# Split weights w1 and w2: the second difference on ScalarE and GpSimd instead of VectorE

## The chip, the cores and the metric

The kernel runs on one core of a Trainium2 chip. The core has TensorE (PE in the profile; PEld is its weight load), VectorE (DVE), ScalarE (ACT), GpSimd (POOL) and SyncE (SP, which here only issues DMAs); GpSimd issues DMAs too. Each engine works off its own queue in order and waits for others by semaphores. The metric is device time of one execution, in microseconds (us); lower is better.

## The reference, cut to what matters

A gated linear recurrence per batch and head makes a state and an output y; the outputs, heads side by side, go through a feed-forward block without nonlinearity.

```python
# batch 4, heads 8, seq 768, head_dim 48; d_model 384, d_ff 1024
scale = np.minimum(mag, 0.999) / (mag + 1e-06)          # mag = |a|
for t in range(S):
    new_re = ar * S_re - ai * S_im
    new_im = ar * S_im + ai * S_re
    S_re, S_im = (new_re + kv, new_im)                  # kv = outer(k_t, v_t)
    y[:, :, t] = np.einsum('bhd,bhde->bhe', q[:, :, t], S_re)
...
a = x @ w1
b = x @ w2
h = a * b @ w3
return h @ w_out
```

## The kernel before

The 3072 tokens are cut into eight units of 384 (unit u is half of batch u // 2). For a unit the kernel works out the gates (`gates`, `gates_apart`: logarithms, exponentials, scans over time, arctangent, sine and cosine, on ScalarE and VectorE in turn), multiplies them into k and q (gR, k, gA, q: the names of the tiles), and moves the results by DMA into KL and QL, where real and imaginary parts lie beneath each other. Then come, per chunk of 128 tokens, transposes (`turn`, tile tp, copied to KT by ScalarE), the state's products (`state`, tile kv, summed into T), the scores (`scores`, tile sc, copied to A under a mask) and the outputs (`outputs`, tile y). The state's products wait for both KT copies of their chunk. The feed-forward of a unit (`ffn_ab`, tiles m and ab; `ffn_out`, tiles o and ot; w3o is w3 times w_out, made once) runs on TensorE between the pieces of the next unit. In ffn_ab each of eight column blocks ends in one product of a and b on VectorE (L1105, called an ab product below).

For units 0 to 2, x times w1 and w2 is done in full float32. For units 3 to 7 x, w1 and w2 are each cut into two words of a faster type (float32r), and a product is done as heads, tails and a correction by differences. The weights are cut once, in `split_ops`, while unit 3 is worked on and unit 2's feed-forward ends: for each of eight blocks i a head (wh, ScalarE, L1152), a tail (low[:, 0], VectorE, L1155) and a difference (low[:, 1], VectorE, L1157). A head is written into the room of the block before it (ws), so it waits for that block's tail. x is cut in `outputs` (x0 on ScalarE, x1 on VectorE, x2 on GpSimd, L1051).

The order of instructions on ScalarE, VectorE, GpSimd and SP in most of the program is set by a planner that runs when the program is built: `run` walks through TensorE's list, and `fill` takes the next piece of the gates, of the weights' cutting or of the input checks where a clock for each engine, kept from the costs in the `yield` lines, says that it fits. The costs are only for the planner. What has been planned stands in each engine's queue in that order. GpSimd's queue also holds the checks of the inputs (`check_weights`; tiles look, seen, looked), of which those left at the end are tested on VectorE and counted by TensorE shortly before the last outputs, and the DMAs of k, q and vr for the next unit. The gates' im is loaded by SP's queue, after the moves' first part for the unit before.

The planner's rule for the cutting:

```python
while (splitting and splitting[0][0] and gate["u"] > THREE and split_t[0] < whole[0] // 2 * 2 and
       start(splitting[0][0]) <= clock["PE"] + 4.0):
    split_next()
while looks and ("ab", 0, KF - 1) in last and clock["POOL"] < min(clock["PE"], split_at(k) - HOLD):
    clock["POOL"] = max(clock["POOL"], clock["PE"] - 4.0) + next(looks[0], 1e9)
```

Of the kernel before, what the change touches and what calls it, by code (L numbers as in the profile page):

```python
# [17 lines left out]
AF = mybir.ActivationFunctionType  # L18
OP = mybir.AluOpType
# [359 lines left out]
def kernel(  # L379
# [36 lines left out]
    nc = tc.nc  # L416
# [22 lines left out]
    TOP, BITS = 1.0 - 2.0 ** -13, 2.0 ** 12  # L439
# [702 lines left out]
    def split_ops():  # L1142
        which = [(n, m) for n in range(FF // WB) for m in (1, 0)]
        for i, (n, m) in enumerate(which):
            yield "ACT", 0.85, ("head", i), (("tail", i - 1),) if i else ()
            w = w_t[n][m]
            if i:
                h = w12.tile([P, KD, WB], FR, tag="w%d%d" % which[i - 1], name="wh")
            else:
                h = late[0].tile([P, KD, WB], FR, tag="x0", padded_shape=[P, KD, TT], name="wh")  # L1150
            w3_h[n, m] = h
            nc.scalar.activation(out=h, in_=w, func=AF.Copy, scale=TOP * BITS)  # L1152
            L = w3_l[n, m] = late[0].tile([P, 2, KD, WB], FR, tag=f"low{n}{m}", name="low")
            yield "DVE", 1.12, ("tail", i), (("head", i),)
            nc.vector.scalar_tensor_tensor(out=L[:, 0], in0=w, scalar=BITS, in1=h, op0=OP.mult, op1=OP.subtract)  # L1155
            yield "DVE", 1.12, ("diff", i), (("tail", i),)
            nc.vector.scalar_tensor_tensor(out=L[:, 1], in0=h, scalar=1.0 / BITS, in1=L[:, 0], op0=OP.mult, op1=OP.subtract)  # L1157
            if i == len(which) - 1:
                yield "ACT", 0.85, ("head", 0), (("tail", i),)
                h = w12.tile([P, KD, WB], FR, tag="w%d%d" % which[i], name="wh")  # L1160
                nc.scalar.activation(out=h, in_=w3_h[which[0]], func=AF.Copy)
                w3_h[which[0]] = h
            split_t[0] += 1
# [573 lines left out]
    with tc.manual_schedule(engines={mybir.EngineType.PE}):  # L1737
# [32 lines left out]
        with tc.manual_schedule(engines={mybir.EngineType.Activation, mybir.EngineType.DVE, mybir.EngineType.Pool, mybir.EngineType.SP}):  # L1770

            paced.append(True)
            clock.update(PE=0.0, ACT=0.0, DVE=0.0, POOL=0.0, SP=3.0, DMA=8.0)
            landings[:] = [0.0] * RING
            ready.clear()
            ready.update({"moves": 9.0, ("raw", 0): 0.0, ("re", 1): 2.0})
            w12_load(0, slice(len(got) and got[0][0][0].stop, KD))
            turn_v(0)
            w12_load(1)
            rest = ffn(0)  # L1780
            urgent.append([None, w12_ops()])

            def head(i):
                if i % 4 == 0:
                    force(i // 4)
                rest[i][1]()
                if i == HEAD - 1:
                    phase.close()
                    late.append(fast.enter_context(tc.tile_pool(name="late", bufs=1)))
                    late.append(fast.enter_context(tc.tile_pool(name="looks", bufs=1)))  # L1790
                    looks.append(check_weights(late[1]))
                    ops = split_ops()
                    splitting.append([next(ops), ops])
            seq = mixed([x for p in pieces(0) for x in p], fills, FILLS[0]) + [("begin", 0)] + [(rest[i][0], lambda i=i: head(i)) for i in range(HEAD)]
            for u in range(1, NU):
                seq += unit(u, rest[HEAD:] if u == 1 else ffn(u - 1), AHEAD[u])
            seq += ffn(NU - 1)
            advance()
            run(seq[:-4] + [("judge", 0)] + seq[-4:-2] + [("judge", 1)] + seq[-2:])
# [41 lines left out]
```

## Time and profile before

| | |
|---|---|
| three timed executions | 534.25, 535.98, 538.77 us; median 535.98 |
| the profiled execution, first to last instruction | 534.5 us (its own device time isn't listed apart from this) |
| mean granted clock of TensorE | 0.993 |
| busy: TensorE, VectorE, ScalarE, GpSimd | 93%, 70%, 61%, 48% |
| the cutting of w1 and w2 | 158 to 180 us |

A row of a timeline gives start, length, engine, line, operation, what is written from what, and in brackets how long the engine had been idle and which work ended that. A line of the page's fifth part gives count, busy time, mean duration and idle time before. Lengths on an engine can overlap by about 0.1 us, since the next instruction starts while the last one drains.

### The profile page before, as it was taken

How to read it: one execution, taken by the hardware profiler on the slowest of the kernel's cores; microseconds unless marked ns; L12 is line 12 of the kernel's file. 1: busy time of each engine (PE TensorE's matmuls, PEld its weight loads, DVE VectorE, ACT ScalarE, POOL GpSimd, SP SyncE). 2: the span in 40 equal slices, each digit the busy share in tenths (PEclk: the TensorE clock that was granted, in tenths of full speed). 3: DMA queues.
4: the chain of work that ended last, by engine and by line, in shares of the span. 5: the costliest groups of instructions: out<-in, count | busy, mean ns of one | idle time of the engine just before them, and what ended most of it. 6: DMA issues, size and time to landing. Idle time of an engine off the chain costs nothing.

```text
span 534.5 us, 13643 instructions
## 1 busy us (share of the span) xinstructions
PE 498.3 (93%) x5594; PEld 378.1 (71%) x5594; DVE 374.7 (70%) x607; ACT 325.6 (61%) x569; POOL 254.0 (48%) x317
## 2 busy tenths in 40 slices
PE   5689889999998999988999999999999998999995
PEld 2355565556655679957888688967896787878972
DVE  7999699855779988756773876577657837336750
ACT  6979866665675458982587557855786554213420
POOL 1000000028968886752664765487457458415510
PEclk9899999999999999998999999999999999999999
DMA  8999859692379219791599239932993176716611
GB/s 258 369 400 286 189 161 307 126 232 72 79 174 229 73 56 234 157 219 40 126 236 216 77 82 245 225 90 70 229 232 87 40 209 169 205 43 189 200 50 37
DMA packets 66424, 89.75 MB, mean 168 GB/s; under 512 B 29872, under 2 KB 53872, under 8 KB 65584
## 3 DMA queue, kind: packets, MB, share of 16 engines
q1 hardware_dynamic: 57904, 59.15, 44.0%
q0 software_dynamic: 8448, 29.63, 20.3%
q8 instruction: 46, 0.75, 0.6%
q14 instruction: 26, 0.21, 0.1%
HBM read 61.01 MB, written 4.72 MB: 123 GB/s over the span
## 4 chain that ended last, share of the span: by engine, by line
PE 51%; DVE 17%; DMA 13%; issue 6%; ACT 5%; POOL 5%; SPq 1%; POOLq 0%; DVEq 0%; ACTq 0%
PE m L1089 24%; PE o L1184 16%; PE y L1043 4%; PE sc L1004 4%; DMA k<-in_k_dram 3%; DMA KL<-k 3%; PE kv L1069 2%; DVE gR L750 2%; PE tp L991 2%; DMA QL<-q 2%; DMA q<-in_q_dram 2%; DMA look<-in_a_re_dram 1%; DVE gA L753 1%; DMA raw<-in_w_dram 1%; POOL look L1327 1%
## 5 line engine op out<-in xcount | busy, mean ns | idle before, releaser
L1184 PE MATMUL o<-w3o,ab 128*128 128x384 f32 x384 | 131.7, 492 | 0.0
L1089 PE MATMUL m<-x,low 128*128 128x384 f32 x576 | 119.2, 339 | 0.0
L1089 PEld LDWEIGHTS m<-x,low 128*128 128x128 f32 x576 | 102.6, 188 | 0.2 <-ACT m L1123 0.2
L1184 PEld LDWEIGHTS o<-w3o,ab 128*128 128x128 f32 x384 | 70.4, 190 | 45.6 <-issue 2.4
L1105 DVE TENSOR_TENSOR ab<-m,ab 128x384 f32<-128x384 f32 x64 | 35.1, 553 | 57.2 <-PE m L1089 39.4
L1089 PE MATMUL m<-x,wh 128*128 128x384 f32 x288 | 69.6, 350 | 3.4 <-ACT ab L1130 2.4
L1123 ACT ACTIVATE m<-m 128x384 f32<-128x384 f32 x96 | 45.5, 476 | 36.0 <-PE m L1089 35.6
L1089 PE MATMUL m<-xT,ws 128*128 128x384 f32 x192 | 63.1, 487 | 1.2 <-ACT xT L1054 1.2
L1328 POOL TENSOR_SCALAR look<-look 128x192 f32<-128x192 f32 (+1 forms) x55 | 54.4, 988 | 5.0
L1089 PEld LDWEIGHTS m<-x,wh 128*128 128x128 f32 x288 | 50.8, 188 | 7.4 <-ACT ab L1130 3.6
L1325 POOL TENSOR_TENSOR look<-look 128x256 f32<-128x256 f32 (+1 forms) x43 | 31.9, 743 | 50.1 <-DMA look<-in_w_dram 32.3
L1089 PEld LDWEIGHTS m<-xT,ws 128*128 128x128 f32 x192 | 36.0, 190 | 25.6 <-ACT xT L1054 1.7
L1273 POOL MEMSET seen<- 128x256 bf16 x1 | 0.3, 317 | 107.7 <-DVE ab L1105 107.7
L1007 DVE COPY_PREDICATED A<-mask,sc 128x512 f32<-128x512 uint8 x48 | 32.8, 734 | 26.5 <-PE sc L1004 26.5
L1289 POOL TENSOR_TENSOR seen<-seen,look 128x192 bf16<-128x192 bf16 (+1 forms) x55 | 44.3, 805 | 4.5
L1051 POOL TENSOR_TENSOR x<-x,x 128x384 fp32r<-128x384 f32 x18 | 23.1, 1284 | 41.7 <-DVE x L1050 41.5
L1188 ACT COPY ot<-o 128x384 f32<-128x384 f32 x24 | 11.4, 476 | 48.4 <-PE o L1184 48.2
L1043 PE MATMUL y<-A,V 128*32 128x128 f32 x768 | 40.2, 276 | 0.6 <-issue 0.6
L1004 PEld LDWEIGHTS sc<-QL,KL 96*32 96x32 f32 x1536 | 29.2, 112 | 13.6 <-issue 8.7
L1004 PE MATMUL sc<-QL,KL 96*32 96x32 f32 (+3 forms) x1536 | 32.8, 238 | 4.4 <-DMA QL<-q 3.0
L1043 PEld LDWEIGHTS y<-A,V 128*32 128x32 f32 x768 | 35.0, 112 | 1.5 <-issue 1.5
L1043 PE MATMUL y<-QL,T 96*32 96x128 f32 x640 | 35.6, 275 | 0.0
(163 smaller groups left out, 909.2 us busy)
## 6 DMA issues: line engine op xcount, KB each, us to landing
looked<-in_w_dram POOLq DMA_DIRECT2D x14, 512.0 KB, 4.5
look<-in_w_dram POOLq DMA_DIRECT2D x27, 256.0 KB, 5.0
raw<-in_w_dram SPq DMA_DIRECT2D x6, 1024.0 KB, 10.3
KL<-gR SPq DMA_DIRECT2D x24, 192.5 KB, 3.6
KL<-k SPq DMA_DIRECT2D x24, 192.5 KB, 7.1
QL<-gA SPq DMA_DIRECT2D x24, 192.0 KB, 8.2
QL<-q SPq DMA_DIRECT2D x24, 192.0 KB, 7.9
raw<-in_w_dram SPq DMA_DIRECT2D x6, 768.0 KB, 6.1
```

Of the source, the lines that this page charges most:

```text
L1004: nc.tensor.matmul(out=sc[SB * g:SB * g + SB, j, s0:C], lhsT=KL[:, x * n + j, w][:, s0:s0 + SB], rhs=QL[:, x * n + j, w][:, s0:C], start=T ...
L1007: last["sc", u, c, x] = nc.vector.copy_predicated(out=A[:, x * n:(x + 1) * n], data=sc, mask=mask)
L1043: nc.tensor.matmul(out=o, lhsT=a, rhs=b, start=s0, stop=s1)
L1051: nc.gpsimd.tensor_tensor(out=x[2], in0=x[1], in1=x[0], op=OP.subtract)
L1089: nc.tensor.matmul(out=out, lhsT=a, rhs=b, start=start and i == 0, stop=i == len(terms) - 1, skip_group_check=not start)
L1105: last["ab", u, j] = nc.vector.tensor_tensor(out=ab_t[u][:, j], in0=m, in1=ab_t[u][:, j], op=OP.mult)
L1123: nc.scalar.activation(out=got[m], in_=got[m], func=AF.Copy, scale=1.0 + 1.0 / BITS)
L1184: nc.tensor.matmul(out=m, lhsT=ab_t[u][:, f, t * P:(t + 1) * P], rhs=w3o[:, f], start=(f == 0), stop=(f == KF - 1))
L1188: nc.scalar.copy(out=o, in_=m)
L1289: nc.gpsimd.tensor_tensor(out=seen[:, 0:n], in0=seen[:, 0:n], in1=x, op=OP.add)
L1325: tt(out=x, in0=x, in1=x, op=OP.mult)
L1328: ts(out=x, in0=x, scalar1=low, scalar2=None, op0=OP.is_ge)
```

## The change

The difference low[:, 1], which is head / 2^12 minus tail, was one VectorE instruction. Now ScalarE writes head / 2^12 into low[:, 1], and GpSimd subtracts the tail from it in place. The planner gets a cost for each (0.85 for ScalarE, 2.6 for GpSimd), in place of 1.12 for VectorE, and so plans the work around it anew.

```diff
             nc.scalar.activation(out=h, in_=w, func=AF.Copy, scale=TOP * BITS)
             L = w3_l[n, m] = late[0].tile([P, 2, KD, WB], FR, tag=f"low{n}{m}", name="low")
+            yield "ACT", 0.85, ("small", i), (("head", i),)
+            nc.scalar.activation(out=L[:, 1], in_=h, func=AF.Copy, scale=1.0 / BITS)
             yield "DVE", 1.12, ("tail", i), (("head", i),)
             nc.vector.scalar_tensor_tensor(out=L[:, 0], in0=w, scalar=BITS, in1=h, op0=OP.mult, op1=OP.subtract)
-            yield "DVE", 1.12, ("diff", i), (("tail", i),)
-            nc.vector.scalar_tensor_tensor(out=L[:, 1], in0=h, scalar=1.0 / BITS, in1=L[:, 0], op0=OP.mult, op1=OP.subtract)
+            yield "POOL", 2.6, ("diff", i), (("tail", i), ("small", i))
+            nc.gpsimd.tensor_tensor(out=L[:, 1], in0=L[:, 1], in1=L[:, 0], op=OP.subtract)
```

TensorE's order stays as it was, instruction for instruction; that of the others moves. Lines from 1155 on have other numbers in the changed program: a small copy is L1155, a tail L1157, a subtraction L1159, and what follows has two more than before.

VectorE in the cutting. Before, its end: the last two tails (L1155), each followed by its difference (L1157), with a sum into the state T between, and then the first product of the gates of unit 4 (im by re):

```order
L1155 SCALAR_TENSOR_TENSOR low<-ws,wh 128x768
L1157 SCALAR_TENSOR_TENSOR low<-wh,low 128x768
L1075 TENSOR_TENSOR T_123<-kv,T_122 96x8x48
L1155 SCALAR_TENSOR_TENSOR low<-ws,wh 128x768
L1157 SCALAR_TENSOR_TENSOR low<-wh,low 128x768
L645 TENSOR_TENSOR im<-im,re 128x384
```

VectorE in the changed program, the beginning of the cutting (L1157 is a tail here):

```order
L1105 TENSOR_TENSOR ab<-m,ab 128x384
L1157 SCALAR_TENSOR_TENSOR low<-ws,wh 128x768
L645 TENSOR_TENSOR im<-im,re 128x384
L1157 SCALAR_TENSOR_TENSOR low<-ws,wh 128x768
L1105 TENSOR_TENSOR ab<-m,ab 128x384
L1157 SCALAR_TENSOR_TENSOR low<-ws,wh 128x768 x2
```

The gates' first product has moved from behind the eighth tail to behind the first.

ScalarE in the same place, before, from the second head (L1152) to the second KT copy, with ab copies (L1101) between:

```order
L1152 ACTIVATE wh<-ws 128x768
L1101 COPY ab<-m 128x384
L1152 ACTIVATE wh<-ws 128x768
L993 COPY KT<-tp 128x128x3
L1101 COPY ab<-m 128x384
L1152 ACTIVATE wh<-ws 128x768
L993 COPY KT<-tp 128x128x3
```

and in the changed program, with the small copies (L1155):

```order
L1152 ACTIVATE wh<-ws 128x768
L1101 COPY ab<-m 128x384
L1155 ACTIVATE low<-wh 128x768
L1152 ACTIVATE wh<-ws 128x768
L1155 ACTIVATE low<-wh 128x768
L993 COPY KT<-tp 128x128x3
L1101 COPY ab<-m 128x384
L1152 ACTIVATE wh<-ws 128x768
L1155 ACTIVATE low<-wh 128x768
L993 COPY KT<-tp 128x128x3
```

The two KT copies stand behind the same heads as before, and each behind one small copy more of the block at hand. The same copies, with the last ones, stand later for the third chunk.

GpSimd. Before, between the loads of k, q and vr for unit 3 and those for unit 4, nine checks of the inputs stood ahead of x2 of unit 3; the last of them and what follows:

```order
L1325 TENSOR_TENSOR look<-look 128x256
L1328 TENSOR_SCALAR look<-look 128x256
L1289 TENSOR_TENSOR seen<-seen,look 128x256
L1051 TENSOR_TENSOR x_1880<-x_1879,x_1878 128x3x128 x3
L527 DMA k<-in_k_dram 128x3x384
L527 DMA q<-in_q_dram 128x3x384
L569 DMA vr<-in_v_dram 128x3x384
```

In the changed program four checks stand there, the end of the fourth here, and then the eight subtractions (L1159):

```order
L1332 TENSOR_TENSOR look<-look 128x192
L1291 TENSOR_TENSOR seen<-seen,look 128x192
L1159 TENSOR_TENSOR low<-low 128x768 x8
L1051 TENSOR_TENSOR x_1867<-x_1866,x_1865 128x3x128 x3
L527 DMA k<-in_k_dram 128x3x384
L527 DMA q<-in_q_dram 128x3x384
L569 DMA vr<-in_v_dram 128x3x384
```

Five checks have moved behind the loads for unit 4, and so all later ones back; at the program's end 13 groups of w3's words are left behind the last x2 instead of 11.

VectorE in unit 4, where the gates' angles are summed (L686) and k is scaled (L702), as the difference of the two programs (- before, + changed):

```order
-L686 SCALAR_TENSOR_TENSOR gZ<-im,st_ang 128x384
-L1105 TENSOR_TENSOR ab<-m,ab 128x384
-L686 SCALAR_TENSOR_TENSOR gZ<-im,st_ang 128x384 x2
-L1105 TENSOR_TENSOR ab<-m,ab 128x384
+L686 SCALAR_TENSOR_TENSOR gZ<-im,st_ang 128x384 x3
 L691 COPY st_ang<-gZ 128x9
 L702 TENSOR_TENSOR k<-k,gR 128x384
```

The gates of unit 4 stand two ab products earlier: five ab products were ahead of the first product for the moves (L750, gR from k), three are now.

## Rows read from the trace of the kernel before

**Rows 1.** The page, its head and part 1

```profile
span 534.5 us, 13643 instructions
...
PE 498.3 (93%) x5594; PEld 378.1 (71%) x5594; DVE 374.7 (70%) x607; ACT 325.6 (61%) x569; POOL 254.0 (48%) x317
...
```

**Rows 2.** Timeline of TensorE, 150 to 262 us: start, length, instruction, idle time before

```profile
...
164.74 2.10 PE L1089 MATMUL m<-xT,ws 128*128 128x384 f32 x6
169.01 0.88 PE L1069 MATMUL kv<-vr,KT 128*32 128x48 f32 x48 [2.17 <-ACT KT L993]
...
174.50 0.88 PE L1069 MATMUL kv<-vr,KT 128*32 128x48 f32 x48
...
181.28 0.88 PE L1069 MATMUL kv<-vr,KT 128*32 128x48 f32 x48
...
235.75 2.85 PE L1184 MATMUL o<-w3o,ab 128*128 128x384 f32 x8
241.58 1.32 PE L1004 MATMUL sc<-QL,KL 96*32 96x128 f32 x64 [2.98 <-DMA QL<-q]
...
```

**Rows 3.** Stretches of 1 us, TensorE alone: length, busy, granted clock, DMA share, GB/s

```profile
...
243.00:244.00 1.00, 0.79 (x29) 0.72 0.00 0
244.00:245.00 1.00, 1.00 (x40) 0.50 0.00 0
...
246.00:247.00 1.00, 1.00 (x31) 0.57 0.08 16
...
```

**Rows 4.** SP's issues, DMA landings around each (last number), and VectorE's timeline

```profile
...
161.31 1.06 SPq L527 DMA_DIRECT2D im<-in_a_im_dram  x1
...
im<-in_a_im_dram SPq DMA_DIRECT2D x1, 576.0 KB, 7.2
...
223.54 0.60 SPq L527 DMA_DIRECT2D im<-in_a_im_dram  x1
...
im<-in_a_im_dram SPq DMA_DIRECT2D x1, 576.0 KB, 8.9
...
232.54 0.56 DVE L645 TENSOR_TENSOR im<-im,re 128x384 f32<-128x384 f32 x1 [0.72 <-DMA im<-in_a_im_dram]
...
```

**Rows 5.** Timeline of VectorE, 150 to 260 us, and line L1157 with its durations

```profile
...
161.85 0.94 DVE L1155 SCALAR_TENSOR_TENSOR low<-ws,wh 128x768 fp32r<-128x768 f32 x1
...
163.99 1.30 DVE L1155 SCALAR_TENSOR_TENSOR low<-ws,wh 128x768 fp32r<-128x768 f32 x1
...
179.97 0.69 DVE L645 TENSOR_TENSOR im<-im,re 128x384 f32<-128x384 f32 x1
...
L1157 DVE SCALAR_TENSOR_TENSOR low<-wh,low x8: 943/980/1235, 162.8 to 179.1; 128x768 fp32r<-128x768 f32 x8
...
```

**Rows 6.** Timeline of ScalarE, 150 to 260 us

```profile
...
167.67 0.84 ACT L1152 ACTIVATE wh<-ws 128x768 fp32r<-128x768 f32 x1 [0.71 <-DVE low L1155]
168.42 0.54 ACT L993 COPY KT<-tp 128x384 f32<-128x384 f32 x1
...
```

**Rows 7.** Timeline of GpSimd, 140 to 320 us, and line L1051 (min/median/max ns)

```profile
...
163.32 1.15 POOL L1289 TENSOR_TENSOR seen<-seen,look 128x192 bf16<-128x192 bf16 x1
...
L1051 POOL TENSOR_TENSOR x<-x,x x18: 989/1066/1663, 193.8 to 480.5; 128x384 fp32r<-128x384 f32 x18
...
```

**Rows 8.** The page, part 5, VectorE's products for ab

```profile
...
L1105 DVE TENSOR_TENSOR ab<-m,ab 128x384 f32<-128x384 f32 x64 | 35.1, 553 | 57.2 <-PE m L1089 39.4
...
```

**Rows 9.** Timeline of VectorE, 150 to 260 us, gates of unit 4

```profile
...
213.26 0.54 DVE L1105 TENSOR_TENSOR ab<-m,ab 128x384 f32<-128x384 f32 x1
...
219.92 0.68 DVE L750 TENSOR_TENSOR gR<-k,re 128x384 f32<-128x384 f32 x1
...
```

**Rows 10.** Timelines of GpSimd and VectorE at the end

```profile
...
508.23 1.04 POOL L1358 TENSOR_TENSOR looked<-looked 128x512 f32<-128x512 f32 x1 [1.54 <-DMA looked<-in_w_dram]
511.20 1.04 POOL L1358 TENSOR_TENSOR looked<-looked 128x512 f32<-128x512 f32 x1 [1.93 <-DMA looked<-in_w_dram]
...
523.17 0.15 DVE L1481 SCALAR_TENSOR_TENSOR count<-count,consts 1x7 f32<-1x7 f32 x1 [5.61 <-PE count L1479]
...
```

## The prediction

> **What bounds the kernel now.** I read the page first: TensorE is busy 93% of the span, the other engines 48 to 70% [rows 1]. A change to VectorE, ScalarE or GpSimd therefore moves the end only through a wait that it takes from TensorE or gives to it. So I went through TensorE's own timeline in the stage of the change and the one after it [rows 2]. The reader is to see two idle places. In the stage where w1 and w2 are split, TensorE ends a product at 166.84 us and starts the first kv product at 169.01, 2.17 us later, because the second copy into KT stood on ScalarE behind a head (wh) that waited for VectorE [rows 6]. In the next unit it ends an output product at 238.60 and waits 2.98 us for QL, the last of the rows that are moved by DMA; right after that the granted clock falls to 0.50 [rows 3], which costs 0.28 + 0.50 + 0.50 + 0.43 = 1.7 us of work (the row at 245 reads as the one at 244). Together 4.7 us hang on the gates of unit 4 being ready sooner. That is what a lighter VectorE can win.
>
> **What is removed and added.** Eight VectorE passes of 0.98 us go, 7.8 us of that engine [rows 5]. ScalarE gets eight copies at the price of the head beside them, 0.84 us each [rows 6], 6.7 us. GpSimd gets eight subtractions of 768 columns. The nearest row is its subtraction of 384 columns in the same type: 0.99 us at least, 1.07 in the median, 1.66 at most [rows 7]. Twice that is 2.0 to 3.3 us; I take 2.0 for one that nobody holds up and count the holding up apart. No wait of TensorE rests on any of these sums: what matters is the order in which the waits fall.
>
> **The new wait.** In the change VectorE's second instruction of the stage is no longer a difference but the first product of the gates of unit 4 (im by re), put between the first and the second tail. It needs all of im, whose DMA is issued at 161.31 and takes 7.2 us to land [rows 4]: 168.5. That this is how a landing is read can be tested on the next unit: 223.54 + 8.9 = 232.44, and VectorE, which says there that it waited for im, starts at 232.54 [rows 4]. Before, the same product ran at 179.97 [rows 5], when im had long been there. Now VectorE stands idle from the end of the first tail, 161.85 + 0.94 = 162.8, to 168.5. Behind the waiting instruction stands the second tail. For it waits ScalarE's third head (it takes the room of the word that the tail reads), and behind this head, in ScalarE's queue, stand a small copy and the two KT copies for which TensorE waits.
>
> **GpSimd and VectorE in each other's way.** The trace shows a second cost. GpSimd's addition of 163.32 lasts 1.15 us, to 164.47; the tail that VectorE starts at 163.99 lasts 1.30 us instead of 0.94, so it got going 0.36 us late, at 164.35, about when GpSimd ended [rows 5, 7]. VectorE's product for ab, which has one operand in PSUM, takes 553 ns on the mean of 64 whatever GpSimd does [rows 8]. I read this as: of a tail and a GpSimd pass one waits until the other is done. The looks in GpSimd's queue are short, so it cost a few tenths; a subtraction of 2.0 us is long. The Trainium skill says the same in SBUF — State Buffer, section Who interferes with whom: a VectorE instruction with two SBUF inputs contends with a GpSimd instruction that reads SBUF, and the one that comes second blocks for the whole instruction. By that rule the sum is the +6.7 us below; no row here shows a wait as long as 2 us, and with the largest excess seen on a tail, 0.4 us, it would be +4.1, the first rival.
>
> **The stage worked out.** While VectorE stands idle GpSimd is through its looks and into the first subtraction when im lands: that holds the im product up by 0 us (done) to 2.0 (just begun); I take 1.2, so it starts at 169.7 and, 0.56 us alone [rows 4], ends at 170.2. Second tail, 0.94: 171.15. Then head three on ScalarE (to 172.05) beside the second subtraction (to 173.2); the third tail, which needs that head, must wait for the subtraction and ends at 174.15. Meanwhile ScalarE does the small copy, the first KT copy and an ab copy; then the fourth head, 0.84 (175.0), the small copy (175.9) and the second KT copy, 0.54 [rows 6]: 176.4. kv starts there instead of at 169.01: **+7.4 us**. Without the blocking the second tail would end at 170.0, the third at 171.9, the second KT copy at 174.7: +5.7 us.
>
> TensorE will then have been idle for 9.6 us. After 2.98 us of idleness it was at half clock until about 246.6, 5.0 us from its start at 241.58 [rows 2, 3]. Bounds: the 1.7 us of that dip, and 2.5 us if all of the first 5.0 us go at half clock. I take **+2.2**, since the fall can only come earlier here.
>
> On to the second kv product (5.5 us of TensorE's work later [rows 2]): 184.1 with the clock; the chain of heads, tails and subtractions, carried on in the same way, has its KT copies ready at 183.8 and hides there. The third stood 6.8 us behind the second, 190.9. Its last KT copy now comes after the eighth tail, the copy of head one and two more small copies: with one subtraction between two tails that is about 192.0: **+1.1**. All subtractions are through by 193. What stands behind them in GpSimd's queue, x2 of this unit and then the loads of k, q and v for the next, waits for TensorE's y, which comes after that; so they are as late as TensorE is and no later. Should a subtraction take 3.3 us, the eight end 10 us later, about when y is there.
>
> **What is given back.** In unit 4 the change's VectorE order has the first product for the move (gR from k, L750) after three ab products instead of five. Before, the third ab was at 213.26 and gR at 219.92 [rows 9], so gR can come some 6 us sooner against TensorE. The V moves stand ahead of it on SP; what is left is about 4 us, and the wait at 241.58 was 2.98. So the wait and its clock dip should go: **-4.7**. What is late next: VectorE's fifth ab product stands behind four products for the moves (0.4 us), and the next unit's im product again stands ahead of two ab products, its DMA landing about when they are due (0.3 us of 0 to 2): **+0.7**.
>
> **The end.** GpSimd's pacing puts the subtractions ahead of the input checks, so four or five looks at w3 fall into the last stage, as two more groups after the last x2 there. Groups come 2.97 us apart, the last starts at 511.20, and VectorE then idles 5.61 us before TensorE's count of the results [rows 10]. Two groups cost 5.9 us against that cover of 5.61. I take nothing, since no ab product is left then to keep VectorE from its tests, and up to 2 us for the upper end, if the loads land later.
>
> **Sum.** 7.4 + 2.2 + 1.1 + 0.7 - 4.7 = +6.7 us. The profiled execution spans 534.5 us [rows 1], 1.5 below the median of the three runs, 535.98, and the sum is made against its rows; it is added to the median: 542.7 us.
>
> **Rivals.** *The blocking is small.* GpSimd's subtraction slows a tail by no more than the 0.4 us seen. Then 5.7 + 2.2 + 0 + 0.7 - 4.7 = +3.9, with a few tenths on the tails +4.1: about 540.1. For it: GpSimd's passes that I saw blocked were no longer than 1.7 us. Against it: the pair at 163.32 and 163.99 fits to 0.1 us.
>
> *The gain of unit 4 does not come.* The moves are bound by the DMA queues rather than by gR, or the later v load holds them. Then +11.4: 547.4.
>
> *Faster (the other side).* If im were in place when asked for, there would be no stall: decided at 163.5, when VectorE would reach the second tail; im would have to land in 2.2 us instead of 7.2. Then the 2.17 us at the first kv product go too, as the KT copies stand behind one head less, and the waits of unit 4: 0.7 - 2.2 - 4.7 = -6.2, 529.8. Against it stand both landings of im that I read; nothing in the change makes the DMA earlier.
>
> **How the numbers follow.** Forecast 0.50, small blocking 0.26, no gain in unit 4 0.17, faster 0.07. The three runs of before differ by 0.8%, so about 1% (530.6 and 541.3) is what a measurement can tell from none. Around its 542.7 the forecast reaches from 539.5 (clock 1.7, shorter subtractions) to 545.5 (the tail, im later); seven tenths of it lie above 541.3. With the third rival all and the first a fifth: 0.35 + 0.17 + 0.05 = 0.57 slower. Faster by over 1% 0.06, the rest, 0.37, within. The range leaves out the faster case and the top of the third rival: 537 to 547.5.
>
> **What would show it.** In the changed profile: VectorE idle some 5.7 us at about 163, ended by the DMA of im; TensorE's wait for KT of 8 to 10 us at about 167, with a clock near 0.5 behind it; tails of 1.3 to 2.9 us instead of 0.94 beside subtractions of 2 us; no wait for QL in unit 4. The prediction is wrong if im is waited for by nobody, if TensorE passes the first kv product as before, or if unit 4 still waits for its moves.

## The result, and the profile after

The changed kernel takes 543.28 us in the median of eight executions, the kernel before 538.06 us in eight beside them; the ratio is 1.0113, with a 95% interval of 1.0068 to 1.0159. The ratio leaves out executions in a slower state, which the medians include. So it is about 1.1% slower. The forecast was 542.7; as the kernel before took 2.1 us more in these runs than in the three that the forecast was added to, the step itself is +5.2 us between the medians (+6.1 by the ratio), against +6.7. One of my names needs mending first: the code's threshold between full float32 and split words is 2, so the weights are cut while unit 2 is worked on and the gates beside it are unit 3's. What the text above calls unit 3, unit 4 and the next unit are units 2, 3 and 4, and full float32 is used for units 0 and 1 alone; I keep the names of the text, so that the steps can be compared.

The profiled execution of the changed kernel took 547.3 us, some 4 us more than the median one. The page's head and part 1, to be held against [rows 1]:

```profile
span 545.5 us, 13651 instructions
...
PE 502.8 (92%) x5594; PEld 380.1 (70%) x5594; DVE 370.4 (68%) x602; ACT 332.2 (61%) x577; POOL 242.3 (44%) x309
```

VectorE has lost 4.3 us and not 7.8 (a pass that is held up counts as busy), ScalarE has gained 6.6, and TensorE, whose work is the same, is busy 4.5 us longer: work at half clock counts as busy. TensorE's timeline, against [rows 2]:

```profile
165.35 2.10 PE L1089 MATMUL m<-xT,ws 128*128 128x384 f32 x6
175.75 1.50 PE L1069 MATMUL kv<-vr,KT 128*32 128x48 f32 x48 [8.30 <-ACT KT L993]
...
177.87 4.02 PE L1089 MATMUL m<-xT,ws 128*128 128x384 f32 x6
...
184.09 0.88 PE L1069 MATMUL kv<-vr,KT 128*32 128x48 f32 x48
...
190.87 0.88 PE L1069 MATMUL kv<-vr,KT 128*32 128x48 f32 x48
...
246.68 2.85 PE L1186 MATMUL o<-w3o,ab 128*128 128x384 f32 x8
249.46 1.32 PE L1004 MATMUL sc<-QL,KL 96*32 96x128 f32 x64
...
361.26 1.32 PE L1004 MATMUL sc<-QL,KL 96*32 96x128 f32 x64 [1.67 <-DMA QL<-q]
```

The wait for KT has grown from 2.17 to 8.30 us; the same product of six parts that takes 2.10 us takes 4.02 behind it; and in unit 4 the scores at 249.46 follow the output product with no bracket at all, so the wait for QL is gone. Another wait for QL, 1.67 us, stands two units later, where there was none. TensorE's granted clock (third number) in the stretch behind the wait, and in unit 4 where [rows 3] had its dip:

```profile
171.00:172.00 1.00, 0.00 (x0) 0.75 1.12 212
172.00:175.00 3.00, 0.00 (x0) 0.50 0.97 196
175.00:180.00 5.00, 4.25 (x55) 0.50 0.02 5
...
181.00:182.00 1.00, 1.00 (x5) 0.63 0.00 0
...
245.00:250.00 5.00, 5.00 (x90) 1.00 0.28 92
```

From 172 to past 181 us TensorE had the lower of its two levels, 1.2 GHz. VectorE in the stage, against [rows 5], with im's issue on SP and its landing against [rows 4]:

```profile
161.98 0.94 DVE L1157 SCALAR_TENSOR_TENSOR low<-ws,wh 128x768 fp32r<-128x768 f32 x1
168.69 1.17 DVE L645 TENSOR_TENSOR im<-im,re 128x384 f32<-128x384 f32 x1 [5.76 <-DMA im<-in_a_im_dram]
169.78 0.94 DVE L1157 SCALAR_TENSOR_TENSOR low<-ws,wh 128x768 fp32r<-128x768 f32 x1
...
171.63 1.86 DVE L1157 SCALAR_TENSOR_TENSOR low<-ws,wh 128x768 fp32r<-128x768 f32 x1 [0.44 <-ACT wh L1152]
174.40 1.85 DVE L1157 SCALAR_TENSOR_TENSOR low<-ws,wh 128x768 fp32r<-128x768 f32 x1 [0.91 <-ACT wh L1152]
176.18 0.55 DVE L1105 TENSOR_TENSOR ab<-m,ab 128x384 f32<-128x384 f32 x1
176.65 1.98 DVE L647 CUSTOM_DVE_ANT_0 gZ<-im 128x384 f32<-128x384 f32 x1
```

```profile
161.81 1.11 SPq L527 DMA_DIRECT2D im<-in_a_im_dram  x1
...
im<-in_a_im_dram SPq DMA_DIRECT2D x1, 576.0 KB, 6.8
```

161.81 + 6.8 = 168.6, and VectorE starts at 168.69. GpSimd and ScalarE beside it, against [rows 7] and [rows 6]:

```profile
167.64 1.80 POOL L1159 TENSOR_TENSOR low<-low 128x768 fp32r<-128x768 f32 x1
170.87 1.81 POOL L1159 TENSOR_TENSOR low<-low 128x768 fp32r<-128x768 f32 x1 [1.43 <-DVE low L1157]
173.64 1.81 POOL L1159 TENSOR_TENSOR low<-low 128x768 fp32r<-128x768 f32 x1 [0.96 <-DVE low L1157]
```

```profile
170.76 0.84 ACT L1152 ACTIVATE wh<-ws 128x768 fp32r<-128x768 f32 x1 [5.85 <-DVE low L1157]
...
175.15 0.54 ACT L993 COPY KT<-tp 128x384 f32<-128x384 f32 x1
...
182.31 0.57 ACT L993 COPY KT<-tp 128x384 f32<-128x384 f32 x1
...
190.12 0.54 ACT L993 COPY KT<-tp 128x384 f32<-128x384 f32 x1
```

The eye should go to the ends. The subtraction of 170.87 ends at 172.68; the tail that started at 171.63 ends at 173.49, 0.81 us later, and alone a tail takes 0.94. The next pair (173.64 and 174.40) repeats it. The ab product between, with one operand in PSUM, keeps its 0.55 us. The three KT copies shown are the last ones ahead of the first, second and third kv product.

### The profile page after: what moved, and what is told of

It reads as the page before. It is cut to its first block, busy times and chain, and to the rows that moved or that the text cites. A ratio compares the mean times of both kernels' runs of the same rounds, so it can differ in the third digit from the quotient of the medians.

```text
span 545.5 us, 13651 instructions
## 1 busy us (share of the span) xinstructions
PE 502.8 (92%) x5594; PEld 380.1 (70%) x5594; DVE 370.4 (68%) x602; ACT 332.2 (61%) x577; POOL 242.3 (44%) x309
## 4 chain that ended last, share of the span: by engine, by line
PE 49%; DVE 18%; DMA 12%; issue 7%; ACT 6%; POOL 5%; SPq 1%; POOLq 0%; ACTq 0%; DVEq 0%
PE m L1089 20%; PE o L1186 15%; DMA k<-in_k_dram 4%; PE sc L1004 4%; PE y L1043 3%; PE kv L1069 2%; DMA im<-in_a_im_dram 2%; PE f L1453 2%; PE tp L991 2%; DMA QL<-q 2%; DMA KL<-k 1%; DMA q<-in_q_dram 1%; DMA look<-in_a_re_dram 1%; DVE gR L750 1%; DVE gA L753 1%
## 5 line engine op out<-in xcount | busy, mean ns | idle before, releaser
L1186 PE MATMUL o<-w3o,ab 128*128 128x384 f32 x384 | 133.3, 497 | 0.0
L1089 PE MATMUL m<-xT,ws 128*128 128x384 f32 x192 | 65.0, 498 | 1.7 <-ACT xT L1054 1.7
L1051 POOL TENSOR_TENSOR x<-x,x 128x384 fp32r<-128x384 f32 x18 | 22.2, 1232 | 64.6 <-DVE x L1050 64.6
L1330 POOL TENSOR_SCALAR look<-look 128x192 f32<-128x192 f32 (+1 forms) x52 | 48.7, 936 | 4.7
L1327 POOL TENSOR_TENSOR look<-look 128x256 f32<-128x256 f32 (+1 forms) x40 | 26.8, 670 | 46.2 <-DMA look<-in_w_dram 30.2
L1190 ACT COPY ot<-o 128x384 f32<-128x384 f32 x24 | 11.5, 478 | 51.2 <-PE o L1186 51.2
L1291 POOL TENSOR_TENSOR seen<-seen,look 128x192 bf16<-128x192 bf16 (+1 forms) x52 | 37.4, 720 | 4.3
## 6 DMA issues: line engine op xcount, KB each, us to landing
QL<-gA SPq DMA_DIRECT2D x24, 192.0 KB, 8.1
QL<-q SPq DMA_DIRECT2D x24, 192.0 KB, 7.8
```

The source lines that it names most:

```text
L1051: nc.gpsimd.tensor_tensor(out=x[2], in0=x[1], in1=x[0], op=OP.subtract)
L1089: nc.tensor.matmul(out=out, lhsT=a, rhs=b, start=start and i == 0, stop=i == len(terms) - 1, skip_group_check=not start)
L1186: nc.tensor.matmul(out=m, lhsT=ab_t[u][:, f, t * P:(t + 1) * P], rhs=w3o[:, f], start=(f == 0), stop=(f == KF - 1))
L1190: nc.scalar.copy(out=o, in_=m)
L1291: nc.gpsimd.tensor_tensor(out=seen[:, 0:n], in0=seen[:, 0:n], in1=x, op=OP.add)
L1327: tt(out=x, in0=x, in1=x, op=OP.mult)
```

## The experiments

Times are medians; each ratio is against the kernel before, measured beside it. The medians of the kernel before run from 536.0 to 538.1 us, so kernels of different experiments are best compared by their ratios. To see where time goes I also follow TensorE's place: how much later than in the kernel before it starts the first, second and third kv product of the stage (169.01, 174.50 and 181.28 us there), the output products at 227.6 and 247.9 (behind the scores of unit 4), the kv product at 283.1 and the last output products at 512.5. All are counted from a kv product ahead of the stage (115.53), because executions differ by up to 8 us before that place, whatever the kernel; three of the profiled executions below (im behind all tails, new work spread, old work between) lie 6 to 9 us above their medians for that reason above all.

| kernel | median us | ratio (95%) | kv 1 | kv 2 | kv 3 | 227.6 | 247.9 | 283.1 | 512.5 |
|---|---|---|---|---|---|---|---|---|---|
| the change | 543.28 | 1.0113 (1.0068 to 1.0159) | 6.1 | 8.9 | 8.9 | 10.3 | 5.9 | 7.4 | 10.4 |
| 1 im behind four tails | 543.43 | 1.0103 (1.0048 to 1.0159) | 0.2 | 5.4 | 7.9 | 9.2 | 4.8 | 6.2 | 6.4 |
| 2 im behind all tails | 540.98 | 1.0052 (1.0005 to 1.0098) | 1.0 | 2.4 | 3.0 | 4.9 | 5.4 | 5.2 | 5.4 |
| 3 plan alone, old work | 544.28 | 1.0133 (1.0081 to 1.0186) | 5.3 | 6.9 | 7.1 | 8.5 | 4.1 | 5.7 | 7.4 |
| 4 as 3, im behind four tails | 538.37 | 1.0016 (0.9980 to 1.0052) | -0.5 | 0.4 | 0.4 | 2.3 | -2.2 | -0.7 | 0.9 |
| 5 as 1, short subtractions | 538.22 | 1.0019 (0.9984 to 1.0055) | 0.0 | 1.7 | 1.7 | 3.0 | -1.5 | 0.1 | 0.5 |
| 6 22 needless products | 549.52 | 1.0238 (1.0182 to 1.0293) | 11.9 | 11.9 | 12.4 | 13.8 | 9.8 | 11.1 | 11.5 |
| 7 new work, spread | 543.54 | 1.0110 (1.0064 to 1.0156) | -2.2 | -2.2 | -2.2 | 8.2 | 8.2 | 8.3 | 8.4 |
| 8 old work, spread | 540.60 | 1.0069 (1.0026 to 1.0112) | -2.3 | -2.3 | -2.3 | 1.1 | 3.0 | 2.4 | 2.4 |
| 9 11 needless products | 545.18 | 1.0113 (1.0043 to 1.0183) | 6.8 | 8.1 | 8.9 | 10.2 | 5.7 | 7.0 | 6.3 |
| 10 old work, between | 536.94 | 0.9978 (0.9949 to 1.0007) | -1.6 | -0.8 | 0.3 | 1.7 | -2.7 | -1.1 | 0.4 |

### 1. The changed kernel, im behind the fourth tail

```diff
-            landed((n, u), after, *(() if u in SPLIT else (1, 2.4)))
+            landed((n, u), after, *(() if u in SPLIT else (1, 2.4))); ready[n, u] += 3.0 * ((n, u) == ("im", 3))
```

> The changed kernel with the order alone mended: the planner is told that im of the unit at hand lands 3 us later, so that the gates' im product stands behind the fourth tail on VectorE instead of behind the first; GpSimd, SP and everything after the cutting stand in the changed kernel's order. Theory A (the stall at the first kv product is the wait for im's DMA, carried over to the tails): the wait of 8.3 us falls to 3 or 4 us (1 us more than before, from tails that GpSimd's subtractions hold up), the stretch at half clock goes or shrinks to the size of a dip behind 3 us of idleness, unit 4 keeps its gain of 4.4 us: 543.3 - 5 - 2 = about 536 to 538, the same as before or up to 2 us faster. Theory B (the stall comes from ScalarE's added small copies and GpSimd's blocked tails, and im only stands in the way by chance): the wait at the first kv product stays at 6 us or more, and the time at 541 or more.

A miss. The first wait went, as theory A said (2.35 us), but the time did not fall: 543.43. TensorE's timeline and VectorE's in this run:

```profile
170.73 0.88 PE L1069 MATMUL kv<-vr,KT 128*32 128x48 f32 x48 [2.35 <-ACT KT L993]
...
181.47 1.50 PE L1069 MATMUL kv<-vr,KT 128*32 128x48 f32 x48 [5.18 <-ACT KT L993]
```

```profile
172.14 1.71 DVE L645 TENSOR_TENSOR im<-im,re 128x384 f32<-128x384 f32 x1
173.88 2.05 DVE L647 CUSTOM_DVE_ANT_0 gZ<-im 128x384 f32<-128x384 f32 x1
...
175.86 2.54 DVE L1157 SCALAR_TENSOR_TENSOR low<-ws,wh 128x768 fp32r<-128x768 f32 x1
```

The wait has moved one kv product on. im had landed, but its product, its square and the tail behind them, 2.1 us when nobody holds them up (0.56 + 0.56 + 0.95 in experiment 5), took 6.3 us beside the subtractions (four back to back from 169.13 to 177.59), and the next head and KT copy waited for that tail. Theory A, im alone, falls; so does theory B as I had written it, since the first wait did not stay. Two causes are left, of which each can make the stall, and the next runs part them.

### 2. The changed kernel, im behind all eight tails

The same line with 20.0 in place of 3.0, which also puts the later gates near their old places.

> As the run with im behind the fourth tail, but with im behind all eight tails, where it stood before the change (im's landing is put 20 us later in the planner's clock). The later gates then stand near their old places among the ab products, too. Theory A: no stall from im as in the other run, but the gain of unit 4 is gone, since it came from the gates standing earlier: the wait for QL of about 3 us and the clock dip behind it are back, so 3 to 5 us more than the run with im behind the fourth tail, 540 to 542. Rival: the gain of unit 4 came from the lighter VectorE by itself, whatever the order: the same time as the other run, within 1 us, and no wait for QL.

540.98 us, inside theory A's 540 to 542. The wait at unit 4's scores is back, 3.74 us (the trace puts its end down to an output's DMA):

```profile
253.59 4.00 PE L1004 MATMUL sc<-QL,KL 96*32 96x128 f32 x128 [3.74 <-DMA out_dram<-ot]
```

From the third kv product on nothing is given back (3.0, then 5.4 at 247.9, where the kernels with early gates gain 4.4). It was the order of the gates, and not the lighter VectorE, that took the wait for QL away. The run shows something else besides. All eight subtractions are in it, and four of the tails beside them take 1.5 to 2.6 us; yet the third kv product is only 3.0 us late, against 7.9 in experiment 1. With no product and no square of the gates between the tails the held-up tails cost much less; that is not the only difference, as the subtractions also begin 3 us later against TensorE than in experiment 1.

### 3. The changed plan with the old work

```diff
-            nc.scalar.activation(out=L[:, 1], in_=h, func=AF.Copy, scale=1.0 / BITS)
...
-            nc.gpsimd.tensor_tensor(out=L[:, 1], in0=L[:, 1], in1=L[:, 0], op=OP.subtract)
+            nc.vector.scalar_tensor_tensor(out=L[:, 1], in0=h, scalar=1.0 / BITS, in1=L[:, 0], op0=OP.mult, op1=OP.subtract)
```

> The changed kernel's plan with the old work: the difference is formed by VectorE in one pass right behind each tail as before the change, ScalarE's small copies and GpSimd's subtractions are not there, but the planner books what it booked in the changed kernel, so im's product stands behind the first tail and its difference. Theory A (the order is the cost): the wait at the first kv product is still 5.5 to 7 us more than the 2.2 us of before, less 1 to 2 us than in the changed kernel because no tail is held up and ScalarE has two small copies less; half clock behind it; time 541 to 543. Rival (the new instructions are the cost): the wait falls to 2 to 3 us and the time to that of before or below it.

544.28 us, with none of the new instructions in it. VectorE's timeline, then TensorE's:

```profile
169.23 0.56 DVE L645 TENSOR_TENSOR im<-im,re 128x384 f32<-128x384 f32 x1 [4.98 <-DMA im<-in_a_im_dram]
169.71 0.95 DVE L1156 SCALAR_TENSOR_TENSOR low<-ws,wh 128x768 fp32r<-128x768 f32 x1
```

```profile
174.36 1.50 PE L1069 MATMUL kv<-vr,KT 128*32 128x48 f32 x48 [7.48 <-ACT KT L993]
```

Tails run their 0.95 us, and still TensorE waits 7.48 us. The order alone makes the slowdown; the time is above the range of theory A, 541 to 543. Its 5.3 us at the first kv product stand beside the 5.7 that the prediction had given without blocking.

### 4. The old work, im behind the fourth tail

Experiment 3 with the line of experiment 1.

> The old work in the changed plan, with im behind the fourth tail: differences on VectorE, no small copies, no subtractions, and the gates of unit 4 planned earlier than before the change. Theory A: no stall from im, first kv product as before the change (wait of 2 to 3 us), and most of unit 4's gain of 4.4 us, as long as VectorE's 7.8 us of differences are worked off beside TensorE: 533 to 536, faster than before by 2 to 5 us. Rival (the gain needs the lighter VectorE): the wait for QL is back and the time is that of before, 537 to 539.

The stall is gone, but the gain of 2 to 5 us did not come: 538.37, ratio 1.0016. Unit 4's wait for QL is gone here too, with VectorE as busy as ever: from 227.6 to 247.9 TensorE wins 4.4 us, as in the changed kernel. Then 1.5 us are lost up to 283.1 in small waits for VectorE and ScalarE, and 1.6 us more at a wait for QL two units on.

### 5. As 1, with short subtractions

```diff
-            nc.gpsimd.tensor_tensor(out=L[:, 1], in0=L[:, 1], in1=L[:, 0], op=OP.subtract)
+            nc.gpsimd.tensor_tensor(out=L[:, 1, :, 0:32], in0=L[:, 1, :, 0:32], in1=L[:, 0, :, 0:32], op=OP.subtract)
```

> The kernel with im behind the fourth tail, with GpSimd's subtraction cut from 256 to 32 of the columns of each row block (the rest of the differences is left out, so this part of the result is not computed). ScalarE's small copies stay. In the run with im behind the fourth tail the wait at the first kv product was gone but 5.18 us stood at the second, behind an im product of 1.71 us, a square of 2.05 and a tail of 2.54 where alone they take 0.55, 0.56 and 0.95. Theory A (GpSimd's long passes hold VectorE up): with short ones these three take their lone times, the wait at the second kv product falls from 5.2 to about 1 us, no half clock; the time is that of the old work in this plan, 538 to 539, within 1 us. Rival (ScalarE's eight small copies of 0.84 us in front of the KT copies are the cost): the wait stays at 3 us or more and the time at 541 or more.

538.22 us. By the ratios that is 4.5 us less than experiment 1, for GpSimd passes of 0.39 us instead of 1.81. ScalarE's eight copies are all there, and the ratio is that of experiment 4 (1.0019 and 1.0016), where VectorE forms the differences instead. VectorE, GpSimd, TensorE and the clock in this run:

```profile
170.03 0.56 DVE L645 TENSOR_TENSOR im<-im,re 128x384 f32<-128x384 f32 x1 [0.50 <-DMA im<-in_a_im_dram]
170.62 0.56 DVE L647 CUSTOM_DVE_ANT_0 gZ<-im 128x384 f32<-128x384 f32 x1
...
171.10 0.95 DVE L1157 SCALAR_TENSOR_TENSOR low<-ws,wh 128x768 fp32r<-128x768 f32 x1
```

```profile
172.20 0.39 POOL L1159 TENSOR_TENSOR low<-low 128x96 fp32r<-128x96 f32 x1 [2.20 <-DVE low L1157]
```

```profile
169.44 0.88 PE L1069 MATMUL kv<-vr,KT 128*32 128x48 f32 x48 [2.14 <-ACT KT L993]
...
176.62 0.88 PE L1069 MATMUL kv<-vr,KT 128*32 128x48 f32 x48
```

```profile
171.00:172.00 1.00, 1.00 (x3) 0.50 1.10 220
```

The second kv product waits for nobody. One thing is not as expected: half clock from 170 to past 173 us, behind a wait of only 2.14 us, which is the 1.7 us that it loses between the first and second kv product.

### 6 and 9. Needless products in the wait

```diff
+        if (u, c) == (THREE, 0):
+            idle = ps_m.tile([P, TT], FP, tag="mm", name="idle")
+            for i in range(22):
+                nc.tensor.matmul(out=idle, lhsT=ident, rhs=xT_t[THREE - 1][:, i % KD], start=True, stop=True)
```

Experiment 9 has 11 in place of 22.

> The changed kernel with 22 needless products (ident by parts of xT, into a bank that nobody reads) ahead of the first kv product of the cutting stage, so that TensorE works through the wait for KT instead of standing idle; they take about 7.7 us of the 8.3 us. Theory (the slow stretch behind the wait comes from the idleness): the granted clock stays at 1.00 from 171 to 182, TensorE gains the 2.85 us between the first and the second kv product, and the time falls by 2 to 3 us from the changed kernel's, to 540.5. Rival (the clock falls for another reason, or the next chain of KT copies is as late anyway): the clock row stays near 0.5, or the second kv product waits for its KT copies what the clock gave back, and the time stays at 543.

> The changed kernel with 11 needless products ahead of the first kv product, half as many as in the run with 22, where one took 0.65 us and not 0.35, so that the 22 outlasted the wait by some 6 us. Eleven take 7.2 us of a wait of 8.3 us. Theory (the slow stretch behind the wait comes from TensorE's idleness): granted clock 1.00 throughout 165 to 185, the first kv product where it was, the second 2.85 us earlier than in the changed kernel unless its KT copies are later than that; time 540 to 542. Rival (what the clock gives is taken back by the second kv product's wait for KT, whose chain of heads, tails and subtractions is nearly as late): a new wait of 2 to 3 us there and the changed kernel's time, 543.

In the first I had mis-sized a product: 0.65 us each, so 14.4 us of filling, of which the excess over the wait is lost (549.52). The second fits, though the first kv product came 0.7 us later than in the changed kernel (6.8 against 6.1). TensorE and its clock there:

```profile
173.43 7.26 PE L1068 MATMUL idle<-xT,ident 128*128 128x384 f32 x22
182.43 0.88 PE L1073 MATMUL kv<-vr,KT 128*32 128x48 f32 x48 [1.74 <-ACT KT L993]
...
189.26 0.88 PE L1073 MATMUL kv<-vr,KT 128*32 128x48 f32 x48 [1.28 <-ACT KT L993]
...
196.79 0.88 PE L1073 MATMUL kv<-vr,KT 128*32 128x48 f32 x48 [0.51 <-ACT KT L993]
```

```profile
183.00:184.00 1.00, 1.00 (x28) 1.00 0.00 0
184.00:185.00 1.00, 1.00 (x5) 1.00 0.00 0
```

The clock stays at 1.00 from 168 to 197 us, so the half-clock stretch did come with the idleness; and keeping the clock up wins nothing. The second and third kv product now wait 1.28 and 0.51 us for KT, and the third starts 8.9 us late, as in the changed kernel. The time, 1.0113 of the kernel before, is the changed kernel's. The rival holds: the chain of heads, tails and subtractions sets the third kv product, and TensorE at half clock only used up its slack in the changed kernel.

### 7 and 8. The cutting spread out, with the new and the old work

```diff
-            landed((n, u), after, *(() if u in SPLIT else (1, 2.4)))
+            landed((n, u), after, *(() if u in SPLIT else (1, 2.4))); ready[n, u] += 10.0 * ((n, u) == ("im", 3))
...
-                       start(splitting[0][0]) <= clock["PE"] + 4.0):
+                       start(splitting[0][0]) <= clock["PE"] + 1.0):
```

> The new work (ScalarE's copy, GpSimd's subtraction) in a plan in which the cutting starts a piece only when it fits within 1 us of TensorE's clock instead of 4, and im is planned 10 us later: no KT copy stands behind more than one head, four of the eight blocks come after the state's products, and im's product stands behind the third tail. Theory A (what costs is only what stands in front of the KT copies): both waits for KT fall under 2 us each, no half clock, blocked tails cost VectorE time beside TensorE's work; unit 4 keeps part of its gain; 536 to 540. Rival (eight subtractions of 1.81 us that VectorE's two-operand passes have to wait for cost wherever they stand): the wait moves to the masks, the x words or the first heads of the next feed-forward, 541 or more.

> The same plan as the other run of this pair, with the old work: differences on VectorE, no small copies, no subtractions on GpSimd. Theory A: the KT copies no longer stand behind heads that wait for tails, so the wait of 2.2 us of before goes to under 1 us, and with the gates planned a little earlier part of unit 4's wait for QL goes too: 533 to 537, 1 to 4 us faster than before. Rival (the late blocks of the cutting cost as much at the masks and x words, or the gates come later): 538 to 540.

In both all three waits for KT are gone (2.2 and 2.3 us ahead of the kernel before). With the new work that is lost again behind them, 10.4 us between the third kv product and 227.6: 4.9 of it at the masks (A), which stand behind gates and tails that subtractions hold up (or behind a head that waits for such a tail), and much of the rest by a lower clock behind these waits (0.73 in the mean from 195 to 200 us, 0.79 from 205 to 210). Unit 4's gain is gone as well, for the scores wait 3.38 us there. These are sizes of one execution, which loses 8.4 us behind 115.53, where the ratio gives 5.9. TensorE there, in the run with the new work:

```profile
194.28 2.36 PE L1004 MATMUL sc<-QL,KL 96*32 96x128 f32 x64 [2.17 <-DVE A L1007]
...
206.57 0.43 PE L1043 MATMUL y<-A,V 128*32 128x128 f32 x8 [2.70 <-DVE A L1007]
```

Both rivals hold. The blocking costs wherever it stands, 543.54 us; and with the old work, 540.60, the gates come late and unit 4 waits 4.06 us for QL.

### 10. The old work, between 4 and 8

Experiment 8 with 2.0 in place of 1.0 and im 6.0 later in place of 10.0.

> The old work (differences on VectorE) in a plan between the last two: a piece of the cutting is taken when it fits within 2 us of TensorE's clock, and im is planned 6 us later, behind the third tail. The second KT copy then stands behind three heads instead of four. Theory: the wait of 2.2 us at the first kv product falls below 1 us, the gates stay early enough that unit 4 does not wait for QL, so 534 to 537 and 1 to 3 us faster than before. Rival (TensorE's gain here comes back as waits further on, as in the other old-work plans): 537 to 539, no difference from before.

The first wait for KT falls to 0.61 us, 1.6 us ahead of the kernel before, and 536.94 us, 0.9978 (0.9949 to 1.0007), is the best time of all; it can't be told from the kernel before. Against the changed kernel it is 1.3% faster. The wait for QL two units on is there as in experiments 3 and 4, 1.74 us.

## Why the prediction was right, and where its steps were not

**The wait for im.** Right as a mechanism: landing worked out at 168.5, seen at 168.6; VectorE idle 5.76 us. It came to 6.1 us at the first kv product instead of 7.4: counted from the kv product of 115.53 im landed 0.5 us sooner than worked out, the im product was held up by 0.6 us (1.17 against 0.56) where I took 1.2, and a subtraction took 1.81 us, not 2.0. Experiment 3 shows that the order alone makes this stall.

**The blocking.** Right as a mechanism, and mis-priced. Tails of 1.85 us beside subtractions of 1.81, an ab product unharmed at 0.55: the row of 163.99 [rows 5] had told it. The Trainium skill's rule that the prediction cited (SBUF — State Buffer, Who interferes with whom) agrees with that, and its page Perfetto Trace Analysis, section Optimizing Scalar/DVE Operations, warns that moving work from VectorE to GpSimd might not help, since they share a read port. Here it is measured: 4.5 us of 543 between experiments 1 and 5 by their ratios, from the length of GpSimd's passes alone. What I had wrong is how it adds up. I put 1.7 us of blocking on top of 5.7 us at the first kv product, so that the first rival, small blocking, came out at 540.1. The kernels with one, both or none of the causes are late at the third kv product by (us, with the time):

| | subtractions of 1.81 us | no long subtraction |
|---|---|---|
| im behind the first tail | 8.9 (543.28 us) | 7.1 (544.28 us) |
| im behind the fourth tail | 7.9 (543.43 us) | 0.4 and 1.7 (538.37 and 538.22 us) |
| im behind all eight tails | 3.0 (540.98 us) | 0 (the kernel before) |

With im behind the first tail the wait for its DMA makes nearly the whole delay, and long subtractions add 1.8 us. With im behind the fourth tail there is no such wait, and the subtractions make 7.9 us; the gates' product and square, which stand between the tails, are held up there too (1.71 and 2.05 us in experiment 1). With im behind all tails they make 3.0. So the two causes don't add: as I read the timelines, the same chain through head, tail and KT copy waits for whichever is later. My first rival looks priced too low, for the kernel nearest to its condition (experiment 3, without blocking) is no faster than the change, 544.28 us. But that is not shown: VectorE still forms the differences there, and no run has im behind the first tail with short subtractions.

**The clock.** +2.2 forecast, +2.85 seen between the first and second kv product; but it is no term of its own. Experiment 9 had no half clock, and lost 1.3 and then 0.8 us there by waits for KT. The sentence that the second chain has its KT copies ready at 183.8 and "hides there" held: the last of them ended at 182.88, and the kv product started at 184.09 without a wait; at full clock, as experiment 9 shows, it would not have hidden. The step that failed is the +1.1 at the third kv product. The last KT copy was to be ready at about 192.0 and ended at 190.66, which is 190.0 counted from the kv product of 115.53; 1.4 of these 2.0 us had been won at the first kv product's copy already. TensorE came at 190.87 and waited for nobody, so the term came out as nothing, and the three terms, 7.4 + 2.2 + 1.1 = 10.7, measured 8.9.

**Unit 4.** -4.7 forecast, -4.4 seen; gR (L750) runs right behind the third ab product (223.19 behind 222.72), as the order had said. The third rival, that this gain doesn't come, is out. Experiments 2 and 4 add that the order of the gates did it.

**The small waits.** +0.7 forecast, and the term most mis-sized: 1.4 us up to 227.6 (ab products and copies at 231.05 and 233.52: 0.47 and 0.64), 1.5 from 247.9 to 283.1, and then the scores' wait for QL at 361.26, which seven of the eight kernels with early gates have at 0.2 to 2.2 us and the kernel before has not. In the profiled execution that last wait was followed by a stretch at half clock, which together with it makes most of the 3 us between 283.1 and 512.5; experiment 9, whose time ratio is the same, lost nothing there. By 283.1 the sum was +7.4 against +6.7.

**The end.** Nothing forecast, nothing seen. GpSimd's last group of w3's words, then VectorE's idle time ahead of the count, against [rows 10]:

```profile
527.60 1.05 POOL L1360 TENSOR_TENSOR looked<-looked 128x512 f32<-128x512 f32 x1 [1.82 <-DMA looked<-in_w_dram]
```

```profile
534.28 0.15 DVE L1483 SCALAR_TENSOR_TENSOR count<-count,consts 1x7 f32<-1x7 f32 x1 [1.97 <-PE count L1481]
```

The two groups took 3.6 of the 5.61 us of cover, so 2 us of it are left.

So the total was right by a fair stroke of luck: the stall's terms were 1.8 us too high, the small waits about as much too low.

## What to carry to other kernels

Before moving a pass to GpSimd, look which VectorE passes with two SBUF operands will run beside it, and who waits for them: each pass moved took 0.98 us off VectorE, and the subtraction in its place put 0.9 us onto four of the eight tails (1.6 at most in the experiments), on a chain that TensorE waited for. When work moves between engines under a planner, read what else it moves: an instruction that waits for a DMA, put ahead of a step that others wait for, cost as much here as the change itself. Look also for passes that can be held up and that stand between the links of such a chain: the same subtractions made 7.9 us with the gates' product and square among the tails, and 3.0 without them. Two causes that hold up the same chain don't add, so taking one away may show nothing; undo both, and then each.

## What the runs showed of the hardware that I had not expected

The granted clock after a wait does not follow from the length of the wait alone. It fell to 0.50 behind 2.14 us of idleness in experiment 5, and stayed at 1.00 behind 2.35 us in experiment 1 and 2.17 us in the kernel before, at the same place of the program. Two units on, in front of the scores, the same happened: it fell to 0.50 behind 1.67 us in the changed kernel (from 362.8 to 366 us) and stayed at 1.00 behind 2.16 us in experiment 3. What decides it is not shown. And the fall did not always cost: where TensorE is ahead of what it waits for next, half clock was free (experiment 9 against the change).
